# Maxima moved into the projection slots, one path for the staged keys, and the finished maxima split after the transpose: one change to a transformer block

## The chip, the cores and the metric

The kernel runs on one core of one Trainium2 chip. The metric is the device time of one execution in microseconds. The engines are called by the names of the profile: PE (TensorE; PEld is its weight load), ACT (ScalarE), DVE (VectorE), POOL (GpSimd) and SP (SyncE, which here only issues DMAs). A name with a small q behind it (SPq, ACTq) is the instruction queue of that engine.

## The reference, cut to what matters

Two blocks follow each other on a sequence of 2048 tokens of 640 features: attention with 32 heads of 20, and a gated feed-forward layer of 1728.

```python
h  = x + attention(layernorm(x), wqkv) @ wo     # softmax(q k^T / sqrt(20)) v, full 2048 x 2048 per head
h2 = h + (silu(layernorm(h) @ w_gate) * (layernorm(h) @ w_up)) @ w_down
```

The softmax needs, for every query of every head, the maximum of its 2048 scores. The kernel computes these maxima in a pass of its own.

## The kernel before, in words

**Stages.** The sequence is cut into 4 chunks (c) of 512 tokens, the heads into 8 groups (g) of 4. A *unit* u is one group with one chunk of queries, so there are 32 units. First comes the projection stage, in which q, k and v are made from x and stored to DRAM; then attention, unit after unit, in 16 steps of 128 keys (kt) each; then the feed-forward layer. In every stage the order of the instructions is written out by hand, and each engine works through its queue in that order.

**Slots of the projection stage (lines 567 to 619).** The stage is a list of 72 slots, 18 for each chunk: 10 *blocks* (`query_key`, 128 rows of q or of k in 15 matmuls 128x512, line 445) and 8 *values* (`value`, 15 matmuls 128x320, line 519). In chunk 3 the order is five key blocks, eight values, five query blocks. `keep` takes a finished block out of PSUM (ACT, then DVE for slots below 8 and POOL later), makes a high and a low part of it, for keys of chunks 0 and 1 also the difference of their first and second 256 columns, and stores it to DRAM with DMAs that ACT issues. Near the end of the values `flip` transposes the next chunk of x (line 415, on PE and ACT and POOL).

**Maxima in the projection stage.** While PE projects, it also computes score maxima, in *pairs* (two matmuls 60x512 for two heads, into one of three `ps_wide` tiles of PSUM). There are two kinds:

- `max_pair` (line 176): DVE reduces all 1024 columns in one instruction (line 180).
- `max_halves` (line 188): the right operand holds the second half of the keys and the difference of the halves. ACT takes the relu of the differences (line 193), and two instructions of DVE add it to the scores of the second half and keep the maximum (line 195). Each is followed by a short read of the accumulator.

`max_halves` works on *staged* operands: 512 KB tiles of q or k in four `raw` buffers, which SP loads from DRAM (`stack`, line 148) in the order of a list of items. `load_items` loads the next item when the slot in which it is in DRAM has come and the user of its buffer has finished; an item is used at the earliest two slots after its load was put in the queue (`ready`, line 332). 42 items are staged for 224 pairs. The other 64 pairs, those of units 0, 1 and 2, are `max_pair` on the tiles of attention.

`visit(n)` puts up to n pairs into the queues, the *urgent* ones of unit 0 first. Before, a block of chunks 1 to 3 has visit(2) after its ninth matmul and visit(3) behind it; a value of chunk 0 has nothing within and visit(4) behind; a value of chunks 1 to 3 has visit(1) or visit(2) within and visit(3) behind. What is left over runs at the end (line 619). The first ten blocks use the two `ps_one` tiles of PSUM.

**Maxima in attention.** The remaining maxima are computed with `max_one` (line 204, reduced by DVE at line 210) between the scores (line 960), the exponentials (ACT, line 966) and the weighted sums (line 970). When a unit's maxima are complete, `max_all` reduces them to 16 numbers per query row (line 217, DVE), and POOL splits these into a high and a low part (`both`, lines 221 and 222). Two steps later `max_finish` transposes the result on PE (line 229), ACT copies it out of PSUM (line 231), and SP sends it into rows of the query tile (line 236).

**POOL's other work in attention.** `prepare_weights` (lines 761 to 902) splits the weights of the feed-forward layer: one task is put into the queues in nearly every step from unit 1 on, not for kt 3 and 4, and not in a step in which `max_all` ran (`quiet`). Its loads and stores are issued by SP. POOL also multiplies each unit's output (line 1005).

Of the kernel before, what the change touches and what calls it, by code (L numbers as in the profile page):

```python
# [29 lines left out]
G = 4  # L30
# [14 lines left out]
def tile_block(ctx: ExitStack, tc: tile.TileContext, x, wqkv, wo, wg, wu, wd, out):  # L45
# [30 lines left out]
    def ps_one():  # L76
        return psum.tile([P, CH], F32, name="ps_one", tag="ps_one", bufs=2)
# [135 lines left out]

    def max_all(u):

        neg = stk.tile([P, G * TPC], F32, name="neg", tag="neg", bufs=2)
        nc.vector.tensor_reduce(  # L217
            neg, mxs[u].rearrange("p b h t k -> p (b h t) k"), axis=AX.X, op=ALU.max, negate=True
        )
        ends[u] = stk.tile([P, 2, G * TPC], F32R, name="both", tag="both", bufs=2)  # L220
        nc.gpsimd.tensor_copy(ends[u][:, 0], neg)  # L221
        nc.gpsimd.tensor_tensor(
            out=ends[u][:, 1], in0=neg, in1=ends[u][:, 0].bitcast(F32), op=ALU.subtract
        )

    def max_finish(u):

        m = ps_one()[: 2 * G * TPC, :P]
        nc.tensor.transpose(m, ends.pop(u).bitcast(F32).rearrange("p i n -> p (i n)"), ident)
        m2 = stk.tile([2 * G * TPC, P], F32R, name="m2", tag="m2", bufs=1)  # L230
        nc.scalar.activation(m2, m, AF.Copy)
        for b in range(2):
            for i in range(2):
                row = b * ROW + NPART + i
                first = (2 * i + b) * 2 * TPC
                nc.sync.dma_start(
                    queries[u][row : row + 1].bitcast(F32).rearrange(
                        "r j (t p) -> r (j t) p", t=TPC
                    ),
                    m2[first : first + 2 * TPC, :].bitcast(F32),  # L240
                )

    def in_projections(u, kc, t):
# [29 lines left out]
    with tc.tile_pool(name="pa", bufs=2) as pa:  # L273
# [16 lines left out]


        slot = [0]
        items, place, users = [], {}, {}

        def stored_at(which, g, c):

# [4 lines left out]

        def raw_tile():
            return pa.tile([P, ND, 2 * P], F32R, name="raw", bufs=4)

        def stage(use, which, g, c):
            place[which, g, use] = len(items)
            users[len(items)] = 0
            items.append([which, g, c, None, None])

        def load_items():  # L310
            for n, (which, g, c, loaded, _) in enumerate(items):
# [10 lines left out]
        def staged_keys(g, c, kc):  # L322
            k = place[1, g, (1, 1) if kc else (c, 0)]
            q = place[0, g, c if c or not kc else 2]

            def one(t, pair):
                max_halves(mxs[g * NC + c], items[q][3], items[k][3], pair, t, kc)
                for n in (k, q):
                    users[n] -= 1
                load_items()  # L330

            def ready():
                return all(items[n][3] is not None and slot[0] >= items[n][4] + 2 for n in (k, q))

            pairs = [(t, pair) for t in moved(g * NC + c, kc) for pair in range(2)]
            for n in (k, q):
                users[n] += len(pairs)
            return [(ready, lambda a=a: one(*a)) for a in pairs]
# [12 lines left out]
        for g in range(1, NG):  # L351
            stage((0, 0), 1, g, 0)
            stage(0, 0, g, 0)
        for g in range(1, NG):
            stage((1, 1), 1, g, 1)
            stage(2, 0, g, 0)
            stage(1, 0, g, 1)
            stage((1, 0), 1, g, 0)
        urgent = [a for kc in range(NC) for a in in_unit(0, kc, 18 * kc + 7)]
        early = [a for g in range(1, NG) for a in staged_keys(g, 0, 0)]  # L360
        early += staged_keys(1, 0, 1) + in_unit(1, 0, 28) + in_unit(1, 1, 28)
        early += [
            a for g in range(1, NG) for c, kc in ((0, 1), (1, 1), (1, 0))[g == 1 :]
            for a in staged_keys(g, c, kc)
        ]
        early += in_unit(2, 0, 46) + in_unit(2, 1, 46)

        def visit(n):
            load_items()
# [69 lines left out]
        def query_key(c, m):  # L439

            z_hi, z_lo = zs[c]
            ps = ps_one()
            for n, (a, w) in enumerate(((z_hi, w_hi), (z_lo, w_hi), (z_hi, w_lo))):
                for k in range(ND):
                    nc.tensor.matmul(  # L445
                        ps, w[:, k, m * P : (m + 1) * P], a[:, k, :],
                        start=(n == 0 and k == 0), stop=(n == 2 and k == ND - 1),
                    )
                    if n == 1 and k == 3 and c:
                        visit(2)  # L450
            keep(c, m, ps)

        halved, firsts = [], []
# [57 lines left out]
        def value(c, t, half):  # L511
            z_hi, z_lo = zs[c]
            ev = evs[t % 2]
            ps = ps_one()[:, :HALF]
            cs = slice(2 * D + half * HALF, 2 * D + (half + 1) * HALF)
            n = 0
            for a, w in ((z_hi, w_hi), (z_hi, w_lo), (z_lo, w_hi)):
                for k in range(ND):
                    nc.tensor.matmul(  # L519
                        ps, a[:, k, t * P : (t + 1) * P], w[:, k, cs],  # L520
                        start=(n == 0), stop=(n == 3 * ND - 1),
                    )
                    n += 1
                    if n == 9 and c:
                        visit(1 + half)
            dst = ev[:, half * 4 : half * 4 + 4, : G * VW].rearrange("p g (h w) -> p g h w", h=G)
            nc.scalar.activation(
                dst[:, :, :, :DH], ps.rearrange("p (g h d) -> p g h d", g=4, h=G), AF.Copy
            )
            if half == 1:  # L530
                rows = slice((c * TPC + t) * P, (c * TPC + t + 1) * P)
                store((v_d[rows], ev))
            else:
                store()
# [32 lines left out]
        for c in range(NC):  # L567
# [7 lines left out]
            for j, (kind, *which) in enumerate(work):  # L575
# [11 lines left out]
                if which:  # L587
# [446 lines left out]

    extra = []
    preparing = prepare_weights()
    quiet = [0]
    for u in range(NU):
        g, c = divmod(u, NC)
        if g == NG - 1 and c >= 2:  # L1040
# [2 lines left out]
        for kt in range(NT):  # L1043
# [5 lines left out]
            for op in order:  # L1049
# [4 lines left out]
                else:  # L1054
# [615 lines left out]
```

## Time and profile before

| | us |
|---|---|
| median of 3 runs | 2136.11 (2132.66 to 2143.45) |
| the profiled execution | 2140.56 |
| its span | 2138.8 |
| span of the projection stage, from its first instruction to the first scores of attention | 411.3 |
| attention up to where the projection behind it begins to take steps | to about 1494 |

A timeline row gives the start, the length, the engine and line, the operation, out<-in, and how many instructions were merged (x6); in brackets stands the idle time before it and what ended it. A windows row gives for a stretch of the span the busy time of each engine with its instructions, then PEclk (the granted clock as a part of the full one), the share of the DMA engines and GB/s. A waits row gives who waited for what, the total, the number of times and the longest. A row of grouped instructions gives busy time and mean length (ns), then the idle time ahead of them.

### The profile page before, as it was taken

How to read it: one execution, taken by the hardware profiler on the slowest of the kernel's cores; microseconds unless marked ns; L12 is line 12 of the kernel's file. 1: busy time of each engine (PE TensorE's matmuls, PEld its weight loads, DVE VectorE, ACT ScalarE, POOL GpSimd, SP SyncE). 2: the span in 40 equal slices, each digit the busy share in tenths (PEclk: the TensorE clock that was granted, in tenths of full speed). 3: DMA queues.
4: the chain of work that ended last, by engine and by line, in shares of the span. 5: the costliest groups of instructions: out<-in, count | busy, mean ns of one | idle time of the engine just before them, and what ended most of it. 6: DMA issues, size and time to landing. Idle time of an engine off the chain costs nothing.

```text
span 2138.8 us, 36948 instructions
## 1 busy us (share of the span) xinstructions
PE 2073.5 (97%) x12636; PEld 1212.7 (57%) x12636; DVE 1663.6 (78%) x3503; ACT 1432.6 (67%) x2803; POOL 705.0 (33%) x1013
## 2 busy tenths in 40 slices
PE   7799999999999999999999999999999999999999
PEld 5566566533333333333333334335568888888888
DVE  6668767888888878888888888887458766666667
ACT  3544575599999989999999999996753222212221
POOL 2131211134434343434340001001125535564455
PEclk9999999999999999999999999999999999999999
DMA  8463644224343353443532212223137845794542
GB/s 254 144 200 100 183 124 146 81 89 129 127 151 121 124 152 117 142 147 126 172 134 68 49 49 73 53 76 94 32 95 249 290 157 199 276 320 157 184 163 93
DMA packets 195283, 301.42 MB, mean 141 GB/s; under 512 B 47121, under 2 KB 81937, under 8 KB 194073
## 3 DMA queue, kind: packets, MB, share of 16 engines
q1 hardware_dynamic: 181512, 270.21, 39.4%
q10 hardware_dynamic: 13584, 28.85, 4.5%
q8 instruction: 102, 1.67, 0.3%
q14 instruction: 85, 0.69, 0.1%
HBM read 199.88 MB, written 98.30 MB: 139 GB/s over the span
## 4 chain that ended last, share of the span: by engine, by line
PE 82%; DVE 5%; DMA 5%; issue 3%; POOL 2%; ACT 2%; SPq 0%; ACTq 0%; POOLq 0%; DVEq 0%
PE acc L970 22%; PE ps_one L960 14%; PE ps_a L1133 14%; PE ps_max L204 11%; PE ps_b L1227 7%; PE ps_one L445 4%; PE ps_wide L188 3%; PE ps_one L519 3%; DVE mx L180 2%; PE ps_max L698 2%; DVE over L195 1%; PE ps_b L698 1%; DMA k_d<-e 1%; DMA raw<-in_B_w_down 1%; ACT over L193 1%
## 5 line engine op out<-in xcount | busy, mean ns | idle before, releaser
L966 ACT ACTIVATE probs<-ps_one 128x512 f32<-128x512 f32 x2048 | 1059.2, 617 | 69.9 <-PE ps_one L960 46.5
L210 DVE TENSOR_REDUCE mx<-ps_max 128x1 f32<-128x512 f32 x1472 | 924.9, 684 | 133.4 <-PE ps_one L960 96.2
L960 PE MATMUL ps_one<-q_stk,k_stk 62*128 62x512 f32 x2048 | 587.6, 452 | 2.9 <-DVE mx L180 2.9
L970 PE MATMUL acc<-probs,v_stk 128*32 128x512 f32 x4096 | 547.4, 607 | 0.0
L960 PEld LDWEIGHTS ps_one<-q_stk,k_stk 62*128 62x128 f32 x2048 | 252.0, 185 | 428.7 <-ACT probs L966 397.1
L204 PE MATMUL ps_max<-k_stk,q_stk 60*128 60x512 f32 x1472 | 380.0, 426 | 1.4 <-DVE mx L210 1.3
L204 PEld LDWEIGHTS ps_max<-k_stk,q_stk 60*128 60x128 f32 x1472 | 271.5, 187 | 29.2 <-DVE mx L210 4.1
L1348 DVE TENSOR_TENSOR tmp<-ps_a,tmp 128x512 f32<-128x512 f32 x208 | 141.2, 689 | 120.1 <-PE ps_a L1133 94.3
L195 DVE CUSTOM_DVE_ANT_0 over<-ps_wide,over 128x256 f32<-128x256 f32 x448 | 162.1, 420 | 91.1 <-ACT over L193 90.2
L1227 PE MATMUL ps_b<-halves,yp 128*128 128x320 f32 x1032 | 179.3, 308 | 2.0 <-DMA halves<-j_d 1.3
L970 PEld LDWEIGHTS acc<-probs,v_stk 128*32 128x32 f32 x4096 | 80.6, 108 | 177.1 <-issue 168.6
L1227 PEld LDWEIGHTS ps_b<-halves,yp 128*128 128x128 f32 x1032 | 165.1, 188 | 18.6 <-POOL yp L86 1.5
L193 ACT ACTIVATE over<-ps_wide 128x512 f32<-128x512 f32 x224 | 122.0, 599 | 69.8 <-PE ps_wide L188 44.2
L1133 PE MATMUL ps_a<-t,units 128*128 128x512 f32 x624 | 162.7, 396 | 0.0
L1133 PE MATMUL ps_a<-z,units 128*128 128x512 f32 x516 | 133.9, 394 | 0.0
L1133 PEld LDWEIGHTS ps_a<-t,units 128*128 128x128 f32 x624 | 112.5, 188 | 18.8 <-ACT tmp L1361 0.2
L86 POOL TENSOR_TENSOR yp<-y,yp 128x256 fp32r<-128x256 f32 x96 | 60.4, 629 | 188.0 <-ACT yp L85 188.0
L1232 DVE TENSOR_TENSOR h<-ps_b,h 128x320 f32<-128x320 f32 x248 | 110.0, 481 | 6.9 <-PE ps_b L1227 5.4
L188 PE MATMUL ps_wide<-raw 60*128 60x512 f32 x448 | 93.1, 467 | 22.8 <-DVE mx L195 11.6
L1005 POOL TENSOR_TENSOR o<-o,rb 128x512 f32<-128x512 f32 x31 | 39.9, 1286 | 212.5 <-DMA q_stk<-q_d 106.4
L221 POOL CAST both<-neg 128x16 fp32r<-128x16 f32 x32 | 6.6, 206 | 310.6 <-DVE neg L217 248.5
L1133 PEld LDWEIGHTS ps_a<-z,units 128*128 128x128 f32 x516 | 93.1, 187 | 15.9
(180 smaller groups left out, 2273.4 us busy)
## 6 DMA issues: line engine op xcount, KB each, us to landing
units<-w_d SPq DMA_DIRECT2D x186, 256.0 KB
w_d<-stage SPq DMA_DIRECT2D x106, 256.0 KB
halves<-j_d SPq DMA_DIRECT2D x70, 320.0 KB
j_d<-stage SPq DMA_DIRECT2D x42, 320.0 KB
k_stk<-k_d SPq DMA_DIRECT2D x64, 160.0 KB
q_stk<-q_d SPq DMA_DIRECT2D x64, 160.0 KB
rb<-r_d SPq DMA_DIRECT2D x32, 256.0 KB
raw<-k_d SPq DMA_DIRECT2D x42, 160.0 KB
```

The source lines that it names most:

```text
L188: nc.tensor.matmul(ps[:, b, :], q[rows, pair, t * P : (t + 1) * P], k[rows, pair, :], start=True, stop=True,)
L193: nc.scalar.activation(over, ps[:, :, CH // 2 :], AF.Relu)
L195: nc.vector.tensor_tensor_reduce(over[:, b], ps[:, b, : CH // 2], over[:, b], 1.0, LOWEST, ALU.add, ALU.max, mx[:, b, pair, t, kc : kc + 1],)
L204: nc.tensor.matmul(ps, queries[u][rows, pair, t * P : (t + 1) * P], keys[u // NC][rows, pair, kc * CH : (kc + 1) * CH], start=True, stop=True,
L210: nc.vector.tensor_reduce(mxs[u][:, b, pair, t, kc : kc + 1], ps, axis=AX.X, op=ALU.max)
L960: nc.tensor.matmul(ps, keys[u // NC][rows, p, kt * P : (kt + 1) * P], queries[u][rows, p, :], start=True, stop=True,)
L966: nc.scalar.activation(probs[p][:, b, :], ps, AF.Exp, scale=scale)
L970: nc.tensor.matmul(acc[32 * j : 32 * j + 32, :], values[u // NC][:, kt, j * VW : j * VW + 32], probs[j // 2][:, j % 2, :], start=(kt == 0) ...
L1133: nc.tensor.matmul(ps.rearrange("p (t n) -> p t n", t=TPC), w[k][:, i], z[k][:, :, j], start=(first and m == 0), stop=(last and m == len(n ...
L1227: nc.tensor.matmul(ps, a, b, start=(n == 0), stop=(n == len(pairs) - 1))
L1232: nc.vector.tensor_tensor(out=h, in0=ps, in1=h, op=ALU.add)
L1348: add = lambda out, ps, x: nc.vector.tensor_tensor(out=out, in0=ps, in1=x, op=ALU.add)
```

## The change

1. **Where pairs stand.** visit(3) instead of visit(2) within a block of chunks 1 to 3 (three behind it stay); visit(2) within every value and visit(2) behind it, those of chunk 0 included.
2. **One list of staged sets.** The pairs of units 1 and 2 in this stage, until now `max_pair` on the tiles of attention, become `max_halves` on staged operands. `staged(g, sets)` makes the items of a set when they are first named. 50 items are staged for 256 pairs; 32 pairs, those of unit 0, stay `max_pair`. The number of all pairs is 288 as before.
3. **First blocks in wide tiles.** The blocks of slots 2 to 6 use one half of a `ps_wide` tile instead of `ps_one`.
4. **Finished maxima.** POOL's two instructions go. PE transposes the 16 numbers themselves; then ACT makes the high part out of PSUM and DVE subtracts it for the low part (`split`, lines 85 and 86). The four DMAs stay.
5. **No quiet steps.** A task of `prepare_weights` is also put into the step in which `max_all` ran.

```diff
     def max_all(u):
-        neg = stk.tile([P, G * TPC], F32, name="neg", tag="neg", bufs=2)
+        ends[u] = stk.tile([P, G * TPC], F32, name="neg", tag="neg", bufs=2)
         nc.vector.tensor_reduce(
-            neg, mxs[u].rearrange("p b h t k -> p (b h t) k"), axis=AX.X, op=ALU.max, negate=True
+            ends[u], mxs[u].rearrange("p b h t k -> p (b h t) k"), axis=AX.X, op=ALU.max, negate=True
         )
-        ends[u] = stk.tile([P, 2, G * TPC], F32R, name="both", tag="both", bufs=2)
-        nc.gpsimd.tensor_copy(ends[u][:, 0], neg)
-        nc.gpsimd.tensor_tensor(
-            out=ends[u][:, 1], in0=neg, in1=ends[u][:, 0].bitcast(F32), op=ALU.subtract
-        )
 
     def max_finish(u):
-        m = ps_one()[: 2 * G * TPC, :P]
-        nc.tensor.transpose(m, ends.pop(u).bitcast(F32).rearrange("p i n -> p (i n)"), ident)
-        m2 = stk.tile([2 * G * TPC, P], F32R, name="m2", tag="m2", bufs=1)
-        nc.scalar.activation(m2, m, AF.Copy)
+        m = ps_one()[: G * TPC, :P]
+        nc.tensor.transpose(m, ends.pop(u), ident)
+        parts = stk.tile([G * TPC, 2, P], F32R, name="m2", tag="m2", bufs=1)
+        split(m, parts[:, 0], parts[:, 1], nc.vector)
...
+        def staged(g, *sets):
+            found = {}
+            for c, kc in sets:
+                for which, chunk in ((1, kc), (0, c)):
+                    if (which, chunk) not in found:
+                        found[which, chunk] = len(items)
+                        users[len(items)] = 0
+                        items.append([which, g, chunk, None, None])
+            return [
+                a for c, kc in sets for a in staged_keys(g, c, kc, found[1, kc], found[0, c])
+            ]
...
-        early = [a for g in range(1, NG) for a in staged_keys(g, 0, 0)]
-        early += staged_keys(1, 0, 1) + in_unit(1, 0, 28) + in_unit(1, 1, 28)
-        early += [
-            a for g in range(1, NG) for c, kc in ((0, 1), (1, 1), (1, 0))[g == 1 :]
-            for a in staged_keys(g, c, kc)
-        ]
-        early += in_unit(2, 0, 46) + in_unit(2, 1, 46)
+        early = [a for g in range(1, NG) for a in staged(g, (0, 0))]
+        early += staged(1, (0, 1)) + staged(2, (0, 1))
+        early += [a for g in range(3) for a in staged(g, (1, 1), (1, 0))]
+        early += [a for g in range(3, NG) for a in staged(g, (0, 1), (1, 1), (1, 0))]
+        early += staged(0, (2, 1), (2, 0))
...
-            ps = ps_one()
+            ps = ps_wide()[:, 0, :] if slot[0] < 7 else ps_one()
...
                     if n == 1 and k == 3 and c:
-                        visit(2)
+                        visit(3)
...
-                    if n == 9 and c:
-                        visit(1 + half)
+                    if n == 9 and slot[0] > 9:
+                        visit(2)
...
-                visit(4 if 9 < slot[0] < 18 else 3)
+                visit(2 if kind == "value" else 3)
...
-                quiet[0] = now[0]
...
-                    if preparing and u and kt not in (3, 4) and quiet[0] != now[0]:
+                    if preparing and u and kt not in (3, 4):
```

More of the change, by code (lines that the diff above doesn't have):

```diff
@@ L234, in max_finish @@
                 row = b * ROW + NPART + i
-                first = (2 * i + b) * 2 * TPC
+                first = b * 2 * TPC
                 nc.sync.dma_start(
@@ L239, in max_finish @@
                     ),
-                    m2[first : first + 2 * TPC, :].bitcast(F32),
+                    parts[first : first + 2 * TPC, i, :].bitcast(F32),
                 )
@@ L292, in tile_block @@
         slot = [0]
-        items, place, users = [], {}, {}
+        items, users = [], {}
         def stored_at(which, g, c):
@@ L303, in raw_tile @@
             return pa.tile([P, ND, 2 * P], F32R, name="raw", bufs=4)
[L305 to L308, printed above, removed]
         def load_items():
@@ L320, in load_items, with staged_keys @@
                 items[n][3:] = t, slot[0]
-        def staged_keys(g, c, kc):
-            k = place[1, g, (1, 1) if kc else (c, 0)]
-            q = place[0, g, c if c or not kc else 2]
+        def staged_keys(g, c, kc, k, q):
             def one(t, pair):
@@ L349, in in_unit @@
             ]
[L351 to L358, printed above, removed]
-        urgent = [a for kc in range(NC) for a in in_unit(0, kc, 18 * kc + 7)]
-        early = [a for g in range(1, NG) for a in staged_keys(g, 0, 0)]
-        early += staged_keys(1, 0, 1) + in_unit(1, 0, 28) + in_unit(1, 1, 28)
-        early += [
-            a for g in range(1, NG) for c, kc in ((0, 1), (1, 1), (1, 0))[g == 1 :]
-            for a in staged_keys(g, c, kc)
-        ]
-        early += in_unit(2, 0, 46) + in_unit(2, 1, 46)
+        def staged(g, *sets):
[9 more added lines that the diff above has]
+            ]
+        urgent = [a for kc in range(NC) for a in in_unit(0, kc, 18 * kc + 7)]
+        early = [a for g in range(1, NG) for a in staged(g, (0, 0))]
[3 more added lines that the diff above has]
+        early += staged(0, (2, 1), (2, 0))
         def visit(n):
@@ L1036, in tile_block @@
     preparing = prepare_weights()
-    quiet = [0]
     for u in range(NU):
```

## The prediction, as it stood before the result

> **What bounds the kernel now.** I read the page first, then the stages, then what PE waited for in each. On the page PE is busy 97% of the span:
>
> ```profile
> PE 2073.5 (97%) x12636; PEld 1212.7 (57%) x12636; DVE 1663.6 (78%) x3503; ACT 1432.6 (67%) x2803; POOL 705.0 (33%) x1013
> ```
>
> A busy PE can still be late: matmuls that are held up overlap and look long. So I cut the span where the slots begin (first matmul of slots 2, 10, 18, 28, 36, 46, 54, 59, 67), at the start of attention, and at the first step of the last projection:
>
> ```profile
> 23.50:61.84 38.34, 32.22 (x140) 23.66 (x139) 26.92 (x55) 14.39 (x28) 5.04 (x7) 1.00 0.82 250
> 61.84:111.25 49.41, 37.23 (x205) 29.35 (x204) 27.84 (x131) 27.74 (x52) 9.79 (x7) 0.90 0.40 124
> 111.25:168.75 57.50, 54.65 (x227) 35.28 (x226) 37.95 (x151) 27.10 (x47) 18.00 (x14) 0.94 0.71 210
> 168.75:211.56 42.81, 38.39 (x214) 27.75 (x213) 35.10 (x100) 21.86 (x41) 7.75 (x6) 0.96 0.26 83
> 211.56:270.77 59.21, 56.88 (x250) 35.24 (x248) 46.35 (x199) 31.88 (x59) 11.60 (x9) 1.00 0.60 176
> 270.77:311.56 40.79, 38.20 (x215) 27.48 (x213) 28.60 (x148) 30.64 (x57) 7.75 (x6) 0.96 0.43 130
> 311.56:339.59 28.03, 27.94 (x125) 17.41 (x124) 17.78 (x100) 17.57 (x33) 5.15 (x4) 1.00 0.47 142
> 339.59:376.93 37.34, 35.21 (x196) 24.64 (x194) 29.32 (x118) 19.97 (x41) 1.71 (x3) 1.00 0.40 129
> 376.93:411.29 34.36, 29.45 (x132) 17.91 (x132) 28.74 (x76) 12.93 (x24) 6.42 (x5) 0.98 0.44 124
> 411.29:1494.50 1083.21, 1074.40 (x7452) 436.73 (x7453) 934.49 (x1539) 1027.70 (x2018) 316.07 (x525) 0.99 0.36 107
> ```
>
> PE is nearly full in attention and in the block stretches, and idle a quarter of the time in the values of chunk 0 (second row), whose clock is also granted at 0.90. What ends most of its idle time in the projection stage, and in attention:
>
> ```profile
> PE ps_wide L188 <- DVE mx L195: 11.6, 21, 2.8
> ```
>
> ```profile
> PE ps_one L229 <- POOL both L222: 8.8, 3, 3.9
> ```
>
> So there are two targets: pairs that wait for a `ps_wide` tile, and three transposes that wait for POOL. Everything else of attention and all of the feed-forward layer keeps its instructions.
>
> **The unit prices.** A value of chunk 0 with four pairs behind it, one of chunk 1 with one within and three behind, and a block of chunk 2 with 2 + 3:
>
> ```profile
> 77.60 0.99 PE L519 MATMUL ps_one<-w_hi,z_hi 128*128 128x320 f32 x5
> ...
> 82.14 0.50 PE L188 MATMUL ps_wide<-raw 60*128 60x512 f32 x2 [1.18 <-DVE mx L195]
> 82.57 0.66 PE L415 MATMUL ps_one<-ident,xt 128*128 128x128 f32 x4
> 82.98 0.98 PE L519 MATMUL ps_one<-w_hi,z_hi 128*128 128x320 f32 x5
> ```
>
> ```profile
> 202.74 0.97 PE L519 MATMUL ps_one<-w_hi,z_hi 128*128 128x320 f32 x5
> ...
> 206.76 1.00 PE L519 MATMUL ps_one<-w_hi,z_hi 128*128 128x320 f32 x5
> ```
>
> ```profile
> 211.56 1.42 PE L445 MATMUL ps_one<-z_hi,w_hi 128*128 128x512 f32 x5
> ...
> 216.07 1.09 PE L188 MATMUL ps_wide<-raw 60*128 60x512 f32 x6
> 217.09 1.45 PE L445 MATMUL ps_one<-z_hi,w_hi 128*128 128x512 f32 x5
> ```
>
> With four pairs in a row the fourth waits, since there are three tiles: 5.38 us for the slot with its flip. With 1 + 3 nothing waits: 4.02 us. A flip is 0.41. A block with five pairs is 5.53; six matmuls of pairs take 1.02 from start to start, so a pair is 0.34, a block with six 5.87, with four 5.2, with none at most 3.85. The readers:
>
> ```profile
> L195 DVE CUSTOM_DVE_ANT_0 over<-ps_wide,over 128x256 f32<-128x256 f32 x448 | 162.1, 420 | 91.1 <-ACT over L193 90.2
> ```
>
> ```profile
> 201.38 1.70 ACT L193 ACTIVATE over<-ps_wide 128x512 f32<-128x512 f32 x3
> ```
>
> ```profile
> 52.93 3.47 DVE L180 TENSOR_REDUCE mx<-ps_wide 128x2 f32<-128x1024 f32 x3
> ```
>
> A staged pair costs DVE two times 0.36 (162.1 for 448, which overlap), and ACT 0.57; a pair of the old kind costs DVE 1.16.
>
> **The change part by part.** The order of the changed program gives the pairs of every slot: 2 + 2 in each value, 3 + 3 in nearly every block that has staged sets, the last pairs in slot 70, none at the end (before, eight in slot 71, six of them behind its block).
>
> *Slots 2 to 9, first blocks in wide tiles: 38.3 stays.* These are PE's waits there:
>
> ```profile
> PE ps_one L445 <- DVE e L486: 3.5, 2, 1.8
> ...
> PE ps_one L445 <- DVE v_stk L86: 1.2, 1, 1.2
> PE ps_one L445 <- DVE v_stk L486: 0.7, 1, 0.7
> ```
>
> The three L445 rows, 5.4 us, go, but slot 7's pairs then need the tiles of blocks 5 and 6, and these are emptied at ACT's pace, which DMAs hold:
>
> ```profile
> 60.94 0.84 ACT L85 ACTIVATE v_stk<-v_stk 128x768 fp32r<-128x768 f32 x1 [5.26 <-DMA k_d<-e]
> 62.12 2.35 DVE L180 TENSOR_REDUCE mx<-ps_wide 128x2 f32<-128x1024 f32 x2
> ```
>
> DVE begins the first three pairs at 52.93 (row above), behind ACT's copy of block 7, and its last two end at 64.47. An earlier PE changes neither. Bounds: 0 and -5.4 (all its waits); I take 0.
>
> *Slots 10 to 17: 49.4 becomes 37.1.* With 2 + 2 the third pair comes six matmuls of the value after the second, and the gap of 1.18 goes: 4.02 each, plus 0.41 for five flips, 26.2 for slots 12 to 17. Slots 10 and 11 take 15.8 (61.84 to 77.60); they still start against the late DVE (64.47, 2.6 behind their start), so I give them two of 4.02 and that wait, with a little for what it delays: 10.9. ACT's 27.7 us of work (second row) come to 75% of the new time: cover, but thin.
>
> *Slots 18 to 27: 57.5 becomes 59.6.* Three pairs more; slots 25 and 26 get eight old-kind pairs and four new ones, 12.2 us of DVE and some statistics against 11.8 of PE, so 12.8; four of 5.87, one of 4.9, one of 4.5 and two of 3.85 make 53.4. By the same prices the slots before come to 51.3, so 6.2 are lost, most of it in slot 21, where a staged set was late and the clock fell behind it (0.94 in the third row):
>
> ```profile
> 119.82 6.35 SPq L148 DMA_DIRECT2D raw<-k_d  x4
> ```
>
> ```profile
> 133.48 1.19 PE L188 MATMUL ps_wide<-raw 60*128 60x512 f32 x3 [2.21 <-issue]
> ```
>
> The same set is still loaded in slot 19 and used in slot 21, so I keep the loss.
>
> *The other values, slots 28 to 35, 46 to 53, 59 to 66:* 42.8, 40.8 and 37.3 become 34.2, 34.2 (eight times 4.02, five flips) and 33.4 (no flips; eight old-kind pairs in two slots add 0.6 each). They have four pairs each instead of four or five, and in the first group the old-kind ones go. *The other blocks, 36 to 45 and 54 to 58:* 59.2 and 28.0 become 62.0 (nine of 5.87, one of 5.2, 1 for the old-kind pairs, 3 of small waits) and 29.4. *Slots 67 to the end:* three blocks of 5.87, one of 5.2, one of 3.85 and 0.7 for the last copy out of PSUM are 27.4 instead of 34.4; the wait for DVE at the start of attention goes. The stage: -12.3 + 2.1 - 8.6 - 6.6 - 3.9 + 2.8 + 1.4 - 7.0 = -32.1.
>
> *Staged loads:* eight items more (32 DMAs on SP), and 21 times instead of 16 a load gets only its two slots, now 8 to 11 us. Bounds: 0 and 5 us each, the loss in slot 21. The fifteen others are nearest: a wait of PE for such a load shows for slot 21 alone. I take 0.25 each: +5.
>
> *Attention:*
>
> ```profile
> 786.60 0.39 PE L229 MATMUL ps_one<-ident,both 128*32 128x128 f32 x1 [3.93 <-POOL both L222]
> 788.92 1.94 PE L970 MATMUL acc<-probs,v_stk 128*32 128x512 f32 x8
> ```
>
> ```profile
> 438.32 0.26 ACT L231 ACTIVATE m<-ps_one 32x128 fp32r<-32x128 f32 x1
> 438.96 0.69 DVE L210 TENSOR_REDUCE mx<-ps_max 128x1 f32<-128x512 f32 x1 [0.45 <-PE ps_max L204]
> ```
>
> POOL's split stood behind its work for the weights; three times PE waited, 8.8 us in all (second waits row), and behind the longest it ran at half the clock for a while (eight weighted sums in 1.94 us), another 1.6. All of it goes. The new subtract on DVE waits for ACT's copy, which ends at 438.58 here; the maximum behind it could not start before 438.96, since PE was late. The subtract is not in the trace; at ACT's 0.26 for twice the rows, the nearest row, it fits. Without that gap it costs up to one reduce (0.69) in each of 31 units, 21 us. I take +1, near the lower end. The Trainium skill speaks against it: "PSUM — Partial Sum Buffer", section "Engine vs sequencer instructions", calls the queues of ScalarE and VectorE strict FIFO; the row of 438.96 shows such a queue with room in it. The quiet steps and POOL's saved work give nothing: no wait for POOL is left in attention. Sum: -8.8 - 1.6 + 1 = -9.4.
>
> Together -32.1 + 5 - 9.4 = **-36.5 us**. The profiled execution (2140.56: span 2138.8 and 1.8 around it) would come to 2104; it lies 4.5 above the median of the runs, 2136.11, so I predict **2100**.
>
> **The rivals.**
>
> *Staged loads are late (slower).* Place: the 21 sets with two slots. If each costs what slot 21 cost, 5 us with its clock, that is 105: 2136 - 41.5 + 105 = 2200. It decides for slower than before once nine of them do. For: SP issues in order, one load was 13.7 us under way (119.82 to 133.48), and the values that give the time get shorter. Against: loads in the values had no such wait, and DMA is busy only 0.26 to 0.43 there. If a fourth do, five of them, 2120.
>
> *Half of it comes back as small waits.* ACT is three quarters busy in the values, and in the blocks the stores that it issues can wait for DMAs (row of 60.94). If each of the 59 slots from 10 to 70 that hold pairs loses 0.3, 18 us of the gain are gone: 2118.
>
> *VectorE holds the maxima.* As above, 20 us more: 2120.
>
> *The clock.* In slots 10 to 17 it was granted at 0.90, a tenth of 49.4 us, with waits of 1.2 and one of 2.8 (first waits row). If the shorter groups provoke that in all values, a tenth of 102 us is lost again: 2110. The Trainium skill has such a case, "TensorE: Matmul & The Clock Gate", section "A second HAM failure mode: psum-queue depth-cycling": short idle times between groups make the clock oscillate. Here the gaps in question are those that go.
>
> *The wide tiles do shorten slots 2 to 9.* Then 5.4 more go: 2095.
>
> **How the numbers follow.** My forecast with small deviations (2090 to 2110) 0.62; the wide tiles, and loads that cost nothing, 0.12; small waits 0.09, VectorE 0.05, the clock 0.04; loads late in some places 0.05, in enough to be slower 0.03. The range reaches from 2083, the bounds of wide tiles and loads taken together with half of the waits I kept, to 2121. 0.5% is about 10.7 us, what a measurement of this kernel can tell from no change: faster (below 2125) 0.91, same 0.05, slower 0.04.
>
> **What would show it.** In the changed profile: attention's first scores near 380 to 388; PE's gaps of 1.1 in slots 12 to 17 gone and value slots of 4.0 to 4.5; slot 7 still waiting for DVE or ACT; no wait of the transpose for POOL, and none of `max_one` for a DVE behind the subtract; step time in attention 2.12 as before. The prediction is wrong if PE waits for `raw` in many slots, or if the stretches of values stay above 38 us.

## The result and the profile after

| | before | after |
|---|---|---|
| median, four runs each, us | 2136.31 (2132.66 to 2143.45) | 2107.84 (2103.70 to 2110.45) |
| ratio | | 0.9861, 95% interval 0.9830 to 0.9892 |
| profiled execution, its span, us | 2140.56, 2138.8 | 2110.45, 2108.7 |
| first scores of attention, us | 411.29 | 389.51 |
| from there to the end of the span, us | 1727.5 | 1719.2 |

The kernel became 28.5 us faster; 36 were forecast. The page after, first part:

```profile
PE 2066.6 (98%) x12636; PEld 1207.3 (57%) x12636; DVE 1659.5 (79%) x3631; ACT 1445.4 (69%) x2835; POOL 691.2 (33%) x949
```

The same stages, cut at the same matmuls as before (windows of the kernel after; line numbers of the program are 10 lower now, from line 366 of the kernel before on). The first row begins with slot 2; that of the kernel before began 1.70 us ahead of slot 2, where PE stood waiting behind the first blocks:

```profile
22.57:61.25 38.68, 34.17 (x140) 25.91 (x138) 27.42 (x55) 15.16 (x28) 7.09 (x8) 0.91 0.85 263
61.25:97.71 36.46, 35.40 (x207) 25.86 (x205) 26.67 (x130) 27.50 (x51) 7.74 (x6) 1.00 0.49 152
97.71:158.45 60.74, 55.70 (x234) 36.48 (x233) 40.72 (x163) 29.03 (x52) 18.04 (x14) 0.94 0.70 202
158.45:194.18 35.73, 34.78 (x207) 25.31 (x205) 25.99 (x134) 27.69 (x53) 7.74 (x6) 1.00 0.50 162
194.18:258.60 64.42, 61.26 (x269) 37.62 (x267) 52.31 (x233) 36.43 (x69) 11.62 (x9) 1.00 0.58 173
258.60:294.58 35.98, 34.89 (x207) 25.30 (x205) 26.00 (x134) 28.00 (x53) 7.76 (x6) 1.00 0.46 146
294.58:325.78 31.20, 30.48 (x137) 18.96 (x135) 20.98 (x118) 20.11 (x38) 5.14 (x4) 1.00 0.47 143
325.78:360.00 34.22, 33.02 (x188) 23.39 (x186) 27.61 (x109) 18.20 (x37) 1.29 (x1) 1.00 0.41 120
360.00:389.51 29.51, 27.70 (x121) 17.52 (x119) 17.43 (x98) 17.74 (x34) 5.15 (x4) 1.00 0.49 132
389.51:1462.24 1072.73, 1071.00 (x7452) 434.09 (x7453) 943.94 (x1569) 1025.14 (x2019) 305.34 (x466) 1.00 0.37 110
```

The value stages (second, fourth, sixth and eighth row) are now nearly full, with the clock at 1.00. The block stages (third, fifth, seventh) are longer than before, because the pairs that left the values stand there. Attention, the last row, took 1072.73 us for the same 7452 matmuls as 1083.21 before, 10.5 less. What follows it took 646.46 instead of 644.30; the clock was halved there for 3.4 us once more than before. The lengths of the slots beside the forecast:

| slots | 2-9 | 10-17 | 18-27 | 28-35 | 36-45 | 46-53 | 54-58 | 59-66 | 67-end |
|---|---|---|---|---|---|---|---|---|---|
| forecast | 38.3 | 37.1 | 59.6 | 34.2 | 62.0 | 34.2 | 29.4 | 33.4 | 27.4 |
| after | 38.68 | 36.46 | 60.74 | 35.73 | 64.42 | 35.98 | 31.20 | 34.22 | 29.51 |

What PE waited for, in the projection stage (first fence) and in attention (second):

```profile
PE ps_wide L188 <- DVE mx L195: 7.1, 24, 0.9
PE ps_wide L188 <- DMA raw<-q_d: 3.4, 2, 2.0
PE ps_wide L176 <- DVE e L476: 2.7, 1, 2.7
...
PE ps_wide L176 <- DVE v_stk L86: 1.8, 1, 1.8
```

```profile
PE ps_one L950 <- DVE m L86: 1.7, 7, 0.3
PE ps_max L204 <- DVE mx L210: 1.3, 1, 1.3
```

No transpose waits for POOL any more. A value of chunk 0 with a flip, slot 15, now takes 4.59 us (84.51 to 89.10), and no row of it has idle time in brackets. Its two groups of pairs and its flip (timeline of the kernel after, PE):

```profile
86.00 0.73 PE L188 MATMUL ps_wide<-raw 60*128 60x512 f32 x4
...
87.74 1.01 PE L188 MATMUL ps_wide<-raw 60*128 60x512 f32 x4
88.69 0.66 PE L405 MATMUL ps_one<-ident,xt 128*128 128x128 f32 x4
```

A block with six pairs, slot 55, takes 6.21 us (300.83 to 307.04), where the forecast had 5.87. All engines of that slot in one timeline:

```profile
303.09 0.96 PE L188 MATMUL ps_wide<-raw 60*128 60x512 f32 x6
...
304.31 0.42 DVE L195 CUSTOM_DVE_ANT_0 over<-ps_wide,over 128x256 f32<-128x256 f32 x1 [1.58 <-ACT over L193]
...
305.56 0.85 PE L188 MATMUL ps_wide<-raw 60*128 60x512 f32 x4
305.67 0.60 ACT L481 ACTIVATE z_hi<-ps_one 128x512 f32<-128x512 f32 x1 [0.42 <-PE ps_one L435]
...
305.73 0.82 ACTq L426 DMA_DIRECT2D k_d<-e  x2
...
306.61 0.50 PE L188 MATMUL ps_wide<-raw 60*128 60x512 f32 x2 [0.20 <-DVE mx L195]
306.68 1.58 ACT L193 ACTIVATE over<-ps_wide 128x512 f32<-128x512 f32 x3 [0.41 <-DVE mx L195]
```

Two of the trailing pairs go at 305.56. The third needs the tile that the third pair within the block filled; DVE starts on that group at 304.31 and reads for three times 0.69 us, and the last read of its accumulator ends at 306.46; then the tile is free. The row at 305.73 matters later: the two stores stand in ACT's queue between the block's copy (line 481) and the relus of the trailing pairs (line 193).

### The profile page after: what moved, and what is told of

Its sections match the earlier page's. It is cut to its first block, busy times and chain, and to the rows that moved or that the text cites. A ratio compares the mean times of both kernels' runs of the same rounds, so it can differ in the third digit from the quotient of the medians.

```text
span 2108.7 us, 37142 instructions
## 1 busy us (share of the span) xinstructions
PE 2066.6 (98%) x12636; PEld 1207.3 (57%) x12636; DVE 1659.5 (79%) x3631; ACT 1445.4 (69%) x2835; POOL 691.2 (33%) x949
## 4 chain that ended last, share of the span: by engine, by line
PE 87%; DVE 6%; DMA 3%; issue 2%; ACT 1%; ACTq 1%; POOL 0%; SPq 0%; DVEq 0%; POOLq 0%
PE acc L960 24%; PE ps_one L950 15%; PE ps_a L1121 15%; PE ps_max L204 12%; PE ps_b L1215 8%; PE ps_one L509 3%; PE ps_wide L188 3%; PE ps_one L435 3%; DVE over L195 2%; PE ps_max L688 2%; DVE mx L180 2%; PE ps_b L688 1%; DMA halves<-j_d 1%; ACTq L426 1%; ACT over L193 0%
## 5 line engine op out<-in xcount | busy, mean ns | idle before, releaser
L195 DVE CUSTOM_DVE_ANT_0 over<-ps_wide,over 128x256 f32<-128x256 f32 x512 | 184.7, 420 | 82.9 <-ACT over L193 82.8
L193 ACT ACTIVATE over<-ps_wide 128x512 f32<-128x512 f32 x256 | 138.6, 597 | 76.9 <-PE ps_wide L188 32.2
L188 PE MATMUL ps_wide<-raw 60*128 60x512 f32 x512 | 107.6, 468 | 12.3 <-DVE mx L195 7.1
L85 ACT ACTIVATE yp<-tmp 128x512 fp32r<-128x512 f32 x40 | 25.3, 632 | 103.1 <-POOL tmp L1208 103.1
```

The lines of the kernel that those rows point to most:

```text
L188: nc.tensor.matmul(ps[:, b, :], q[rows, pair, t * P : (t + 1) * P], k[rows, pair, :], start=True, stop=True,)
L193: nc.scalar.activation(over, ps[:, :, CH // 2 :], AF.Relu)
L195: nc.vector.tensor_tensor_reduce(over[:, b], ps[:, b, : CH // 2], over[:, b], 1.0, LOWEST, ALU.add, ALU.max, mx[:, b, pair, t, kc : kc + 1],)
```

## The experiments

**What each part is worth.** Five kernels do or undo one part. Times are medians. The kernel before, run beside them on the same chip, had 2135.22 us (beside the first two and the last) and 2133.88 (beside the two in the middle).

| kernel | us | ratio to before, 95% interval |
|---|---|---|
| before plus the maxima's new end | 2125.86 | 0.9957 (0.9942 to 0.9973) |
| after minus the maxima's new end | 2115.67 | 0.9920 (0.9903 to 0.9938) |
| before plus the new places of the pairs | 2123.39 | 0.9945 (0.9930 to 0.9961) |
| before plus key differences for all sets | 2127.71 | 0.9974 (0.9959 to 0.9990) |
| after minus the wide tiles | 2109.46 | 0.9889 (0.9867 to 0.9911) |

*The maxima's new end alone.* Before, with this edit (and `neg` as `ends[u]`, and no `quiet`):

```diff
-        nc.gpsimd.tensor_copy(ends[u][:, 0], neg)
-        nc.gpsimd.tensor_tensor(
-            out=ends[u][:, 1], in0=neg, in1=ends[u][:, 0].bitcast(F32), op=ALU.subtract
-        )
...
+        split(m, parts[:, 0], parts[:, 1], nc.vector)
```

> The kernel before the change, with only the new end of the maxima: transposed first, then split by VectorE, and no tile of weights held back in the tile of scores that follows. If the whole saving of the attention comes from it, this is 8 to 10 us shorter than the kernel before (the attention went from 1727.5 to 1719.2 us from the first scores on), with the projections as before (411.3 us to the first scores). If VectorE's maxima pay for it there, it is less than 4 us shorter. If the attention gained only because the maxima arrive earlier from the projections, it is not shorter at all.

Measured: 9.4 us less (2135.22 to 2125.86). The first theory holds. (The projections have the instructions of the kernel before; in this profile they reach the first scores at 402.8 us, in the profile of before at 411.3. More on that below.) PE's waits in attention, from 404 to 1480 us, in this kernel:

```profile
PE ps_one L955 <- DVE m L86: 1.8, 7, 0.3
```

*The other way round:* after, with the diff's lines of `max_all`, `max_finish` and `quiet` reversed.

> The kernel after the change, with the old end of the maxima put back: split by GpSimd ahead of the transpose, and a tile of weights held back in the tile of scores that follows. If the end of the maxima and the staging of the keys add up without touching each other, the time is 8 to 10 us longer than after the change, all of it behind the first scores. If half of the attention's gain came from the projections leaving less behind, it is 3 to 5 us longer.

Measured: 2115.67, 7.8 us more than after. The wait is back in attention, as long as before the change:

```profile
PE ps_one L229 <- POOL both L222: 8.5, 3, 3.8
```

So the part is worth 8 to 9 us whatever the projections do. The exchange is plain in the two rows: 8.5 us of waits for POOL go, and 1.8 us of waits for DVE's subtract come, because a score's `ps_one` tile is free only when the subtract has read it. That is 6.7 us; behind two of the three waits for POOL this kernel also runs 6.8 us at a clock of 0.50 (from 759.2 and from 1042.5 us). Part 5 of the change, no quiet steps, went with the new end in both kernels and was not tried alone.

*The places alone, and the key differences alone:*

```diff
-                        visit(2)
+                        visit(3)
...
-                    if n == 9 and c:
-                        visit(1 + half)
+                    if n == 9 and slot[0] > 9:
+                        visit(2)
...
-                visit(4 if 9 < slot[0] < 18 else 3)
+                visit(2 if kind == "value" else 3)
```

> The kernel before the change, with only the new places of the pairs: three within and three behind a block's products, two within and two behind a value's. The pairs stay of the old kinds where they were. If the two parts of the change in the projections (places, key differences) add up, the places give 3 to 7 us of the some 19 us that remain when the 9.4 us of the maxima's new end are taken from the 28.5. If a pair of the old kind, 1.16 us on VectorE, binds the slots wherever it stands, the places alone give less than 2 us, and the values still take 4.6 us or more each.

```diff
-        early = [a for g in range(1, NG) for a in staged_keys(g, 0, 0)]
-        early += staged_keys(1, 0, 1) + in_unit(1, 0, 28) + in_unit(1, 1, 28)
...
+        early = [a for g in range(1, NG) for a in staged(g, (0, 0))]
+        early += staged(1, (0, 1)) + staged(2, (0, 1))
...
```

> The kernel before the change, with only the key differences for all staged sets, and the pairs in their old places. If the parts add up, this gives 12 to 16 us against the kernel before. If the trailing three and four pairs in one place bind the slots through the three wide tiles however cheap a pair is on VectorE, it gives less than 8 us, and the rest of the 19 us comes only with both parts together.

Measured: 10.5 us for the places (2133.88 to 2123.39), 6.2 for the key differences. The parts add up (9.4 + 10.5 + 6.2 = 26.1, against 27.4 and 28.5 for the whole), but I had the two sizes the wrong way round: the places probably bring more (by the intervals 8 to 15 us, against 2 to 9), since the values of chunk 0 hold staged pairs already. Slots 10 to 17, one windows row each of the kernel with the places alone, with the key differences alone, and with the maxima's new end alone:

```profile
62.36:98.84 36.48, 35.33 (x205) 25.80 (x205) 26.79 (x130) 27.39 (x51) 7.74 (x6) 1.00 0.49 150
```

```profile
61.74:104.31 42.57, 33.21 (x207) 25.71 (x205) 26.55 (x131) 27.38 (x51) 7.76 (x6) 1.00 0.44 132
```

```profile
60.67:103.40 42.73, 33.36 (x205) 25.79 (x205) 26.78 (x131) 27.40 (x51) 7.77 (x6) 1.00 0.41 132
```

The last two have the instructions of the kernel before in these slots. They take 42.6 and 42.7 us, not 49.4: the profiled execution of before had lost 6.7 us there by its wait of 2.8 and a clock of 0.90. The places themselves are worth 6.2 in this stage.

*The wide tiles undone:*

```diff
-            ps = ps_wide()[:, 0, :] if slot[0] < 7 else ps_one()
+            ps = ps_one()
```

> The kernel after the change, with one part of it undone: the products of the first seven slots go to the two single tiles again instead of the wide ones. If the wide tiles only let TensorE run ahead and wait later for the halves of earlier blocks, as the trace after the change shows in slots 2 to 9 (37.75 us against 38.3 us before), the time stays within 2 us of the kernel after the change, and the stretch at half clock at 46.3 to 53.1 us may move. If the wide tiles are worth something that the waits of slot 7 hide, it is 4 to 8 us longer: eight blocks, half to one us each.

(Five blocks stand in wide tiles, those of slots 2 to 6; the counts in this text are off.) Measured: 2109.46, 1.6 us more than after and inside its spread; the tiles are worth nothing that can be measured. The kernel after shows why. PE runs ahead through slots 2 to 6 at 3.40 us each, and gives it back in slot 7, first fence; then it works at half clock, second fence (two windows; the last but two number is the clock, which fell within the first of them, at 48.4 us):

```profile
43.09 0.77 PE L176 MATMUL ps_wide<-k_stk,q_stk 60*128 60x512 f32 x2
45.66 0.51 PE L176 MATMUL ps_wide<-k_stk,q_stk 60*128 60x512 f32 x2 [1.81 <-DVE v_stk L86]
48.87 0.80 PE L176 MATMUL ps_wide<-k_stk,q_stk 60*128 60x512 f32 x2 [2.70 <-DVE e L476]
```

```profile
46.30:49.70 3.40, 0.83 (x3) 0.40 (x3) 2.41 (x7) 1.42 (x5) 0.00 (x0) 0.81 0.96 274
49.70:53.10 3.40, 3.40 (x8) 2.70 (x9) 2.37 (x3) 1.26 (x3) 2.10 (x3) 0.50 0.97 265
```

Without the wide tiles the same two slots, 7 and 8, run at full clock:

```profile
45.05:49.59 4.54, 4.54 (x22) 3.22 (x22) 2.93 (x11) 2.61 (x5) 0.39 (x1) 1.00 0.92 269
49.59:55.10 5.51, 4.88 (x23) 3.29 (x21) 5.24 (x8) 2.11 (x4) 2.45 (x4) 1.00 0.93 273
```

**Why a block with six pairs takes 6.24 us.** My theory after the result: the third trailing pair waits for the tile of the third pair within the block, so an earlier group within the block removes the wait. Rivals: ACT's work or the switching of PE sets the slot.

*An earlier break:*

```diff
-                    if n == 1 and k == 3 and c:
+                    if n == 1 and k == 1 and c:
```

> The kernel after the change, with one size moved: the three pairs inside a block's 12 matmuls stand after the 6th matmul instead of the 8th, behind which only the trailing three come. If the slots with six pairs take 6.24 instead of the 5.87 us that were summed because VectorE has not read the first wide tiles when the trailing pairs ask for them again, the trailing pairs come later by two matmuls, the wait goes, and the projections get 5 to 9 us shorter (25 such slots, 0.2 to 0.37 us each). If the 6.24 us are the switching of TensorE between kinds of products, or ScalarE's copies, or VectorE's own sum of work in a slot, the time stays within 2 us. If the break so early meets the wide tiles of the slot before, the wait only changes its place: within 2 us as well, with the waits on the pairs inside the block.

(A block has 15 matmuls; the break moves from behind the 9th to behind the 7th. The counts in this text are off.) Measured: 2110.46, 2.6 us more than after. The first theory, as far as it says that this removes the wait, fell. The trace shows where it went; slot 57 of this kernel takes 7.04 us, PE's rows first, then ACT's:

```profile
317.65 0.50 PE L188 MATMUL ps_wide<-raw 60*128 60x512 f32 x2 [0.35 <-DVE mx L195]
318.34 1.24 PE L188 MATMUL ps_wide<-raw 60*128 60x512 f32 x4 [0.19 <-DVE mx L195]
...
321.55 0.96 PE L188 MATMUL ps_wide<-raw 60*128 60x512 f32 x6
```

```profile
314.61 0.60 ACT L481 ACTIVATE e<-ps_one 128x512 f32<-128x512 f32 x1 [1.42 <-PE ps_one L435]
314.67 1.31 ACTq L426 DMA_DIRECT2D k_d<-z_hi  x3
316.10 1.58 ACT L193 ACTIVATE over<-ps_wide 128x512 f32<-128x512 f32 x3 [0.89 <-PE ps_wide L188]
```

The trailing pairs now go in one run (the row at 321.55), but the three pairs within the block wait one after another, for tiles of the trailing pairs *before*. Those are read late, since ACT first issues three stores, 1.31 us, and only then makes the relus (316.10; the matmuls of PE that the brackets name began at 314.50, and the first of these pairs had long ended). Slots 54 and 55 of the same kernel, ahead of whose start no store or one stood there, take 5.77 and 5.90. So there are two chains on the same three tiles, and the second begins in ACT's queue.

*The stores behind the trailing pairs, break at the old place,* and then *both*:

```diff
-            store(*pieces, queue=...)
+            posts.append(lambda: store(*pieces, queue=...))
...
                 visit(2 if kind == "value" else 3)
+                while posts:
+                    posts.pop(0)()
                 finish_keep()
```

> The kernel after the change, with only the stores moved behind the trailing pairs; the pairs within a block stay after its 9th matmul. If the third trailing pair waits for VectorE's reading of the third pair within the block, as the trace after the change shows (0.18 to 0.20 us of gap and the stretched pair before it), the stores are not in that chain, and the time stays within 2 us with slots of 6.24. If ScalarE's queue is what holds the slot as a whole, it is 5 us or more shorter already with this.

> The kernel after the change, with the pairs within a block after the 7th of its 15 matmuls (instead of the 9th), and each block's stores issued by ScalarE's queue behind the trailing pairs instead of ahead of them. The early break alone left the time as it was: its trace shows slots of 5.77 and 5.90 us where ScalarE issued one or no store between the block's copy and the trailing pairs, and of 6.55 to 7.04 where it issued two or three (0.9 to 1.4 us), because the trailing pairs' copies, and with them VectorE, come later by that time and the early break meets wide tiles still unread. If that is the cause, all slots of six pairs take 5.8 to 6.0 here, and the time is 5 to 10 us shorter than after the change. If the wide tiles are short for six pairs in 5.8 us anyway, it is within 2 us.

Measured: 2104.24 and 2102.33 (ratios to before 0.9857, 0.9830 to 0.9884, and 0.9851, 0.9821 to 0.9881). That is 3.6 and 5.5 us below after, less than the intervals tell apart, but the stage does tell them apart. From slot 36 to the first scores, with all pairs of chunks 2 and 3 in it:

| kernel | slot 36 to first scores, us | six-pair slots 54 to 58, us each |
|---|---|---|
| after, and once more | 195.33, 195.63 | 6.21 to 6.28, 6.22 to 6.54 |
| early break alone | 199.51 | 5.77 to 7.04 |
| stores moved alone | 191.69 | 6.24 to 6.27 |
| both | 190.02 | 5.79 to 6.05 |
| both, first blocks in single tiles (the last kernel below) | 189.82 | 5.75 to 6.08 |

Waits for DVE's reading in that stretch, after, and with both edits (with the early break alone they are 6.3 us, with the stores moved alone 3.6):

```profile
PE ps_wide L188 <- DVE mx L195: 5.0, 20, 0.9
```

```profile
PE ps_wide L188 <- DVE mx L195: 1.5, 1, 1.5
```

And ACT's rows at the end of slot 55 with both, which takes 5.92 us with no gap of PE: two of the three relus now start between the copy and the first store:

```profile
308.52 0.60 ACT L481 ACTIVATE z_hi<-ps_one 128x512 f32<-128x512 f32 x1 [1.14 <-PE ps_one L435]
309.01 1.08 ACT L193 ACTIVATE over<-ps_wide 128x512 f32<-128x512 f32 x2
309.56 0.82 ACTq L426 DMA_DIRECT2D k_d<-e  x2
```

With the stores moved alone the six-pair slots stay at 6.24, as expected: there the group within the block sets the wait. What this edit does remove is a delay of the value behind the blocks: slot 59 takes 4.09 instead of 5.09 us. (Slots 28 and 46, the other two of that kind, shrink by 0.19 and 0.37 only.) The two edits together bring the slots near the 5.87 of the forecast. So both chains are shown: with either edit alone the other chain still holds the slots, and with both they are short. That holds for the stretch of the table. The profiled execution with both edits, at 2106.63 us the slowest of its four, lost it again earlier: its slots 10 to 35 took 136.1 us, against 132.9 after.

**The loss in slot 21.** PE waits there 1.39 and 2.04 us for a staged load, and the stretch from 118.0 to 124.8 runs at 0.66 of the clock. I let the two sets concerned be used two slots later, on top of the two edits:

```diff
-    slot[0] >= items[n][4] + 2 for n in (k, q)
+    slot[0] >= items[n][4] + (4 if n in (12, 13) else 2) for n in (k, q)
```

> The kernel after the change with the early break (7th matmul) and the stores behind the trailing pairs, and with one more size moved: the staged set that slot 21 waits for (its loads are issued at 109.7 to 116.3 us and land after 118 us) may be used from the fourth slot after its load on, not from the second, so that slots 21 and 22 go without pairs and slots 23 and 24, which had none, take them. If slot 21's 10 to 12 us are the wait for these loads and the half clock behind it, 3 to 6 us go on top of the 5 us of early break and stores: 2094 to 2100 us, 8 to 13 us below the kernel after the change on the same chip. If slot 21's wait only moves to the next set, or the loads hold the clock low whoever waits, the late set gives nothing: 2100 to 2104 us.

*After once more,* on the same chip:

> The kernel after the change, unaltered, on the same chip as the two runs beside it: its time is what they are compared with. By its first runs 2104 to 2110 us, 26 to 29 us below the kernel before.

Measured: 2105.72 against 2108.02 for the kernel after. The late set gives nothing; the theory fell. Slots 21 and 22 shrink to 3.42 and 3.40 us, but slot 23 takes 9.69 and slot 24 5.71. Slots 21 to 24 come to 22.2 us, against 23.3 and 21.4 in the two profiles of the kernel after. The rows of slot 23, ACT's first, then PE's:

```profile
124.57 1.84 ACTq L426 DMA_DIRECT2D k_d<-e  x3
126.46 0.84 ACT L85 ACTIVATE e<-e 128x768 fp32r<-128x768 f32 x1 [3.34 <-DMA k_d<-e]
127.21 1.55 ACT L193 ACTIVATE over<-ps_wide 128x512 f32<-128x512 f32 x3
```

```profile
124.50 1.30 PE L435 MATMUL ps_one<-z_hi,w_lo 128*128 128x512 f32 x5
128.75 0.50 PE L188 MATMUL ps_wide<-raw 60*128 60x512 f32 x2 [2.94 <-DVE mx L195]
```

Here it is no load. ACT's relus stand behind the three stores of its own queue. The first goes out at 124.57, when POOL's split of what it stores has ended (124.54). The third goes out at 126.11, when, as far as the semaphores tell, the store issued at 121.13 has landed (126.09). The relus, DVE and PE follow. DMA is busy for 0.88 of slot 23. Which transfer one would have to move so that nobody waits in slots 18 to 24 was not tried and stays open.

*Both edits, and the first blocks in single tiles again:*

> The kernel after the change with the early break and the stores behind the trailing pairs, and with the first blocks' products in the single tiles as before the change. In the profile of the early break with the stores moved, the wide tiles let TensorE run ahead to slot 7, which then takes 10.3 us and is followed by a stretch at half clock. If that stall costs what the wide tiles gain, this takes the same time within 2 us as the early break with the stores moved (2100 to 2104 us). If the wide tiles do gain, it is 2 to 4 us longer; if the stall costs more than they gain, 2 to 4 us shorter.

Measured: 2102.75 (2100.43 to 2103.42; ratio to before 0.9846, 0.9822 to 0.9869). The wide tiles again make no difference. It is the fastest here beside the one with both edits alone, 5.3 us below the kernel after on the same chip (2104.55 to 2109.97); the spreads do not touch, though the intervals of the two ratios do. Against the kernel before it saves 32.6 us.

## Why the prediction was right, and where it was 8 us short

- **Places and mechanism: right.** Both targets, the pairs that wait for a `ps_wide` tile and the transposes that wait for POOL, gave a gain, as the profile promised. In the values of chunk 0 the waits for DVE's reading of staged pairs fell from 6.3 to 0.6 us; in the whole stage they fell from 11.6 to 7.1 only, since 3.5 us now stand in the blocks, where 0.8 stood before. A value of chunk 0 comes to 4.43 to 4.60 us with its flip, for which the sum had 4.43. The first scores stand at 389.5 us, just behind the 380 to 388 that were named as a sign, and no stretch of values is above 38.
- **Slots 10 to 17: right for the time after, not for what the change does.** The sum took 12.3 us off a row of 49.41. Kernels with the same instructions there take 42.6. Half of the step, 6.7 us, was the profiled execution of before, not the change. I had seen the sign of it, the clock of 0.90 in that row, and that this execution lay 4.5 us above the median. The sum priced the slots without that loss, so its 2104 no longer held it. The last step, from 2104 to 2100, took it off a second time: as far as the 4.5 us lay in these slots, 4 of the 8 us by which the forecast was short are this step.
- **The mis-sized term: a block with six pairs, 5.87.** The sixth pair was priced at PE's own spacing, 0.34, as if three tiles carried it. It measured 6.24 (6.21 to 6.28 in 14 of the 19 slots with six staged pairs, more in the others), some 0.37 more in each of the 21 slots for which the sum used 5.87: 7.8 us. With the two edits it is 5.8 to 6.0. The first value behind each group of blocks, priced at 4.02, took 5.40 (slot 28), 5.55 (slot 46) and 5.09 (slot 59): another 4.0. The stages from slot 18 on came out 11.6 us longer than summed, and these two terms are 11.8. That they agree so well is partly chance: the sum already held 3 us of small waits, and two blocks with four pairs, priced at 5.2, took 5.58 and 6.33 (slots 39 and 70).
- **Staged loads, +5: not needed.** PE waits for `raw` twice, 3.4 us, both times in slot 21, whose loss stood in the sum already. The term hid nearly half of the one above.
- **Slots 2 to 9: right.** 38.3 forecast, 38.68 measured, and the wait in slot 7 is the one named, on DVE behind ACT's copies. (That DMAs hold ACT shows there in part: between 30 and 50 us ACT waits 4.7 us for DMAs and 7.7 for DVE.) What I did not see is the stretch at half clock behind it.
- **Attention: -9.4 forecast, -10.5 in the two traces, -8.3 with what follows it, 9.4 and 7.8 by the runs.** The subtract cost 1.7 us of PE's waits (+1 taken), by scores that wait for its PSUM tile, not by maxima behind it on DVE, as I had it. The Trainium skill ("PSUM — Partial Sum Buffer", section "Engine vs sequencer instructions") has VectorE's and ScalarE's queues as strict FIFO. That rule, weighed there against DVE, was at work in ACT's queue: three stores ahead of the relus in the trace of the early break, and their move worth what the table shows.
- **The rivals.** Late loads did not come. Small waits did come back, 11.6 of the 18 us priced, though not as 0.3 in every slot but in the block slots and the values behind them, for the reason above; the result lies about midway between the forecast and this rival. VectorE did not hold the maxima. The clock went the other way: 1.00 in all value stages.

## What to carry to other kernels

Price an added piece of work not by its spacing on the busiest engine but by the whole cycle of the buffer that it takes, from the fill to the last read, and look at what else stands in the queue of each engine in that cycle: here two chains of nearly the same length ran over three tiles, and removing one alone made the slots longer or left them as they were. And before a saving is read off a stage, look at its clock: a stage of the kernel before that shows a low clock or one long wait may be shorter in the next execution without any change. That loss may be taken off once, and not again at the end of the sum.

## What the runs showed of the hardware that was not expected

**A fifth to a quarter of the gain goes with the clock.** The mean granted clock was 0.9924 over 13 executions of the kernel before and 0.9955 over four of the kernel after. The part not granted is 0.0076 of 2135 us, 16.2 us, and 0.0045 of 2108 us, 9.5 us: 6.7 of the 28.5 us. This estimate takes PE as at work through all of the time at half clock. Another way gives 5.6: over the 39 executions of the kernel before that were run beside the experiments, 0.001 more clock goes with 1.8 us less time (correlation -0.80). Between kernels the clock alone decides little: without the wide tiles it was 0.9968 at 2109.46 us, with the late set 0.993 at 2105.72. That fewer waits of PE bring the higher clock is what the stretches below suggest; no run here sets the one without the other.

**Short waits are enough to halve it.** The stretches at half clock are 3.4, 6.8 or, in two profiles, 10.2 us long. In slot 7 the clock was 0.50 from 48.4 us on. In the 3.41 us ahead of that PE worked for 0.51 us; its gaps were 1.81 and 2.70 us, and the second was still open when the clock fell. The Trainium skill ("TensorE: Matmul & The Clock Gate", section "Why this matters for your kernels") advises no idle gaps above about 3 us, and its section "What's actually happening" has a window of 3.4 us that runs freely. The lengths of the stretches agree with that window; the limit on the gap does not hold here. With the late set two waits of 0.63 us in slot 43 were enough, with PE at work for 2.06 of 3.41 us (the last but two number is the clock):

```profile
239.42:242.83 3.41, 2.06 (x10) 1.11 (x10) 3.41 (x5) 1.23 (x2) 1.25 (x1) 1.00 0.73 196
242.83:246.24 3.41, 3.41 (x12) 2.01 (x10) 3.28 (x8) 0.00 (x0) 0.02 (x1) 0.50 0.27 102
```

I cut all 13 profiles into such windows, in step with the changes of the clock, without the last 10 us of each. Of those at full clock, all 27 with PE at work for less than 1.6 us were followed by half clock, 28 of the 85 between 1.6 and 2.4 us, and 3 of some 7700 above that. So what counts here is the busy share of the window, not the longest gap.
